# Linear attention and a max-of-three FFN on one core: k of batches 3 to 7 transposed by DMA, q's second chunk packed on ScalarE, batch 3's products a step later

## The chip, the cores and the metric

The kernel runs on one core of one Trainium2 chip. The metric is device microseconds of one execution. Times called "time" are these; a "span" is the length of one execution's trace, about 2 us, at most 3, shorter in these runs. A trace shows one execution. Times are compared within one call, on one chip, with the kernel before run in turn. A ratio is the mean time of one kernel's fast runs over the mean of the other's fast runs of the same rounds, so it is not quite the ratio of the medians that are quoted.

PE is the matmul engine and PEld its weight loads. DVE is VectorE, ACT is ScalarE, POOL is GpSimd and SP is SyncE. SP only issues DMAs here; SPq is its queue.

## The reference, cut to what matters

```python
# q, k, v: (8 batches, 8 heads, 1024, 64); E, F: (64, 1024)
k_proj = einsum('ks,bhsd->bhkd', E, k)          # 64 rows a head instead of 1024
v_proj = einsum('ks,bhsd->bhkd', F, v)
attn   = softmax(q @ k_proj^T / 8)              # (.., 1024, 64)
x      = (attn @ v_proj) as (8192 tokens, 512)
out    = max(x @ w1, x @ w2, x @ w3) @ w_out    # 512 -> 768 -> 512, float32
```

The FFN is nearly all of the PE work. The attention of batch n+1 is spread over the FFN steps of batch n.

## The kernel before

A batch has two chunks of 512 tokens. A chunk has ten steps: six `up` steps of 12 matmuls (about 2.6 us of PE each) and four `down` steps of 6 matmuls (1.3 us). `plan(b)` lists what attention work is put behind which step: `(1, 3)` is chunk 1, step 3. PE's work runs in the order of the program in these traces, so one instruction that waits holds up those that follow: in the changed kernel batch 4's first scores wait 3.25 us, and the `down` matmuls behind them start only after these, at 172.81 us instead of 169.68 before.

The kernel's scores read q and the projected k with the head dimension on the partitions. q gets there by a DMA transpose ("q's turn", 1 MB, issued by SP). k's projection gets there by two PE transposes and a copy out of PSUM:

```python
def load(b, which):                                   # on GpSimd's queue
    tiles = qkv[b] if b in qkv else load_tiles(b)
    for i in which:
        dma = nc.gpsimd.dma_start(out=tiles[i], in_=view((q, k, v)[i], b))
        if i == 0 and b - 1 in last_T:
            after(dma, last_T[b - 1])                 # q's load waits for the previous q turn

def qd(b, parts=1):                                   # pack q on VectorE, turn it by DMA
    def f():
        # ... allocation and packing copies cut
                last_T[b] = nc.sync.dma_start_transpose(out=qTs[b][...], in_=q_p[...])

def kproj(b):
    def f():
        t, ns = bank()
        proj(b, 1, t, (LO, HI), 4 * D)                # 16 matmuls
        kps[b] = att.tile([P, 2, 2 * D], BF16, name="kp")
        copy("v", kps[b].rearrange("a g x -> a (g x)"), t[:, 0:4 * D], ns, 0.43)

def kt(b):                                            # the transposes that the change removes
    def f():
        t, ns = two()
        t = t.bitcast(BF16)[:, 0]
        for gg in range(2):
            nc.tensor.transpose(out=t[:, gg * P:(gg + 1) * P],
                                in_=kps[b][:, gg, :], identity=ident)
        # ... a line cut
        kpTs[b] = att.tile([P, NPAIR, KP], BF16, name="kpT")
        copy("v", kpTs[b].rearrange("a (y x) k -> a x y k", x=2), t[...], ns, 0.3)

# qd: pack and turn q.  sc: scores of a head pair.  za, vx: sums, values.  zc: sums and 1/z, by SP DMAs
# plan(0), cut
(0, 7): [qd(1, 2), za(0, 2, *c1)],
(1, 2): [vproj(1), ld(2)],
# plan(2)
(0, 1): [kproj(3), vproj(3), ld(4)],
(0, 2): [kt(3)],
(0, 3): [sc(3, 0, now=True), sc(3, 1)],
(0, 5): [sc(3, 2, now=True), sc(3, 3)],
(0, 7): [zc(3)],
(0, 8): [qd(4)],
(1, 3): [kproj(4), vproj(4), ld(5), vx(3, 0), vx(3, 1)],
(1, 4): [kt(4)],
(1, 7): [vx(3, 2), vx(3, 3), sc(4, 0)],
# plan(3) and later, n = b + 1: the rest of n's scores at (0, 1), zc(n) at (0, 3), qd(n+1) at (0, 4),
# kproj(n+1), vproj(n+1) at (1, 2), kt(n+1), ld(n+2) at (1, 3), sc(n+1, 0) at (1, 6)
```

The softmax here doesn't subtract the row's maximum and nothing guards it: scores larger than these inputs give would overflow.

Of the kernel before, what the change touches and what calls it, by code (L numbers as in the profile page):

```python
# [9 lines left out]
BF16 = mybir.dt.bfloat16  # L10
# [5 lines left out]
def kernel(  # L16
# [13 lines left out]
    nc = tc.nc  # L30

    B, H, S, D = q.shape
    KP = E.shape[0]
# [4 lines left out]
    P = 128  # L38
# [13 lines left out]
    att = ctx.enter_context(tc.tile_pool(name="att", bufs=2))  # L52
# [55 lines left out]
    def after(dma, earlier):  # L108
        tc.add_manual_dep(
            dma.ins, earlier.ins.name,  # L110
            mybir.DependencyInfo(
                mybir.DependencyClass.Sync, mybir.DependencyReason.DATA
            ),
        )
# [16 lines left out]
    qkv, qTs, kpTs, vps, pTs, zis, xTs = {}, {}, {}, {}, {}, {}, {}  # L131
# [5 lines left out]
    def load_tiles(b):  # L137
        qkv[b] = tuple(
            loads.tile([P, H, SI, D], BF16, name=nm, bufs=n)
            for nm, n in (("q_t", 2), ("k_t", 1), ("v_t", 1))  # L140
        )
        return qkv[b]
# [55 lines left out]
    def load(b, which):  # L198
        tiles = qkv[b] if b in qkv else load_tiles(b)
        for i in which:  # L200
            dma = nc.gpsimd.dma_start(out=tiles[i], in_=view((q, k, v)[i], b))  # L201
            if i == 0 and b - 1 in last_T:
                after(dma, last_T[b - 1])

    def scores(b, g, lo, nsi):
        t, ns = two()
        n = nsi // 2
        for c in range(2):
            for hp in range(2):
                rows = slice(hp * HALF, (hp + 1) * HALF)  # L210
                at = g * SI + lo + c * n
                nc.tensor.matmul(  # L212
                    out=t[c * HALF:(c + 1) * HALF, hp, 0:n * P],
                    lhsT=kpTs[b][rows, g, :],
                    rhs=qTs[b][rows, at:at + n, :],
                    start=True, stop=True,
                )
        return t[:, :, 0:n * P], ns, pe(n * MM / 4 + 0.1)
# [65 lines left out]
    def vx(b, g):  # L284
        def f():
            scale_x(b, g, 0, SI, values(b, g, 0, SI))
        return f
# [34 lines left out]
    def sc(b, g, lo=0, nsi=SI, now=False):  # L322
        def f():
            t = scores(b, g, lo, nsi)
            if now:
                exps(b, g, lo, nsi, t)
            else:
                later.append(lambda: exps(b, g, lo, nsi, t))
        return f
# [34 lines left out]
    q_pk = {}  # L364

    def pack_q(b, gs, lo, nsi):


        def f():
            if b not in q_pk:  # L370
                q_pk[b] = att.tile([P, NPAIR, SI, 2, D], BF16, name="q_p", bufs=1)
            for g in gs:
                copy(
                    "v", q_pk[b][:, g, lo:lo + nsi].rearrange("p si h d -> p h si d"),
                    qkv[b][0][:, 2 * g:2 * g + 2, lo:lo + nsi], (), 0.25,
                )
        return f

# [39 lines left out]
    kps = {}  # L418
# [3 lines that stand above are left out]
            proj(b, 1, t, (LO, HI), 4 * D)  # L422
            kps[b] = att.tile([P, 2, 2 * D], BF16, name="kp")
            copy("v", kps[b].rearrange("a g x -> a (g x)"), t[:, 0:4 * D], ns, 0.43)
        return f

    def kt(b):
# [4 lines that stand above are left out]
                nc.tensor.transpose(  # L432
                    out=t[:, gg * P:(gg + 1) * P], in_=kps[b][:, gg, :], identity=ident
                )
            pe(0.2)

            kpTs[b] = att.tile([P, NPAIR, KP], BF16, name="kpT")
            copy(
                "v", kpTs[b].rearrange("a (y x) k -> a x y k", x=2),
                t[:, 0:2 * P].rearrange("a (x y k) -> a x y k", x=2, y=2), ns, 0.3,  # L440
            )
        return f

    def vproj(b):
        def f():
            t, ns = bank()
            proj(b, 2, t, (LO, HI), 4 * D)

            vps[b] = att.tile([P, H, D], BF16, name="vp")
            for hh, hs in enumerate((LO, HI)):  # L450
                i = t[hh * HALF:(hh + 1) * HALF, 0:4 * D].rearrange("a (h d) -> a h d", d=D)
                for to in range(2):
                    copy("sv"[hh], vps[b][to * HALF:(to + 1) * HALF, hs, :], i, ns, 0.4)
        return f
# [250 lines left out]
    def ld(b, which=(0, 1, 2)):  # L705
        return lambda: load(b, which)

    def plan(b):
        n = b + 1
        if b == 0:  # L710
            c1 = (SPC, SPC)
            return {
                (0, 6): [za(0, 1, *c1), sc(0, 3, *c1)],
                (0, 7): [qd(1, 2), za(0, 2, *c1)],
                (0, 8): [za(0, 3, *c1)],
                (1, 0): [kproj(1)],
                (1, 1): [kt(1)],
                (1, 2): [vproj(1), ld(2)],
                (1, (3, "mid")): [sc(1, 0, now=True), sc(1, 1)],
                (1, 4): [za(1, 0), sc(1, 2, now=True)],  # L720
                (1, 5): [za(1, 1), sc(1, 3)],
                (1, 7): [za(1, 2)],
                (1, 8): [za(1, 3)],
            }
        if b == 1:
            return {
                (0, 0): [qd(2)],
                (0, 3): [kproj(2), vproj(2), ld(3, (0,))],
                (0, 4): [kt(2)],
                (0, 5): [sc(2, 0, now=True), sc(2, 1, now=True), sc(2, 2)],  # L730
                (0, 6): [sc(2, 3)],
                (0, 8): [zc(2, nc.gpsimd), ld(3, (1, 2))],
                (1, 1): [qd(3)],
                (1, 3): [vx(2, 0), vx(2, 1)],
                (1, 6): [vx(2, 2), vx(2, 3)],
            }
        if b == 2:
            return {
                (0, 1): [kproj(3), vproj(3), ld(4)],
                (0, 2): [kt(3)],  # L740
                (0, 3): [sc(3, 0, now=True), sc(3, 1)],
                (0, 5): [sc(3, 2, now=True), sc(3, 3)],
                (0, 7): [zc(3)],
                (0, 8): [qd(4)],
                (1, 3): [kproj(4), vproj(4), ld(5), vx(3, 0), vx(3, 1)],
                (1, 4): [kt(4)],
                (1, 7): [vx(3, 2), vx(3, 3), sc(4, 0)],
            }
        if n == B:
            return {}  # L750
        out = {
            (0, 1): [sc(n, 1, now=True), sc(n, 2, now=True), sc(n, 3)],
            (0, 3): [zc(n)],
            (1, 2): [vx(n, 0), vx(n, 1)],
            (1, 6): [vx(n, 2), vx(n, 3)],
        }
        if n + 1 < B:
            out[0, 4] = [qd(n + 1)]
            out[1, 2] = [kproj(n + 1), vproj(n + 1)] + out[1, 2]
            out[1, 3] = [kt(n + 1)]  # L760
            out[1, 6] += [sc(n + 1, 0)]
        if n + 2 < B:
            out[1, 3] += [ld(n + 2)]
        return out

    for b in range(B):
        p = plan(b)

        def behind(ch, step):
            for f in p.get((ch, step), []):  # L770
                f()

        for ch in range(NCHUNK):
            if (b, ch) == (0, 0):
                c1 = (SPC, SPC)
                up_first({
                    (0, 0, 1): [lambda: x(1)],
                    (0, 0, 3): [lambda: z(2), lambda: z(3)],
                    (0, 1, 3): [lambda: v_pair(2), lambda: x(2)],
                    (0, 1, 5): [lambda: v_pair(3), ld(1)],  # L780
                    (0, 2, 1): [lambda: x(3)],
                    (2, "a", 0): [pack_q(0, (0, 1), *c1)],
                    (2, "a", 1): [pack_q(0, (2, 3), *c1)],
                    (2, "a", 4): [qp(0, (0, 1), *c1)],
                    (2, "a", 5): [qp(0, (2, 3), *c1)],
                    (2, 1): [sc(0, 0, *c1)],
                    (2, 3): [sc(0, 1, *c1)],
                    (2, 4): [za(0, 0, *c1, then=True), sc(0, 2, *c1)],
                })
                run_later()  # L790
                behind(0, NJT - 1)
            else:
                for step in range(NJT):
                    up(b, ch, step, lambda: behind(ch, (step, "mid")))
                    behind(ch, step)
            for tt in range(SPC):
                down(b, ch, tt, "v" if b == 0 else "s")
                behind(ch, NJT + tt)
# [30 lines left out]
```

## Time and profile before

| before | |
|---|---|
| time, median of 3 runs | 401.98 us (401.90 to 402.39) |
| span of the profiled run | 401.0 us |
| PE busy | 392.7 us, 98% |
| VectorE, ScalarE busy | 51%, 37% |
| chain that ended last, share on PE | 84% |

The windows view shows where PE is not busy. Columns: stretch in us from the span's start, its length, busy time of each engine (with the number of instructions), the granted PE clock as a share of full speed, DMA share, GB/s.

```profile
24.00:33.00 9.00, 9.00 (x43) 4.04 (x42) 6.25 (x11) 1.56 (x3) 1.66 (x2) 1.00 1.25 205
33.00:48.00 15.00, 14.08 (x111) 6.09 (x110) 12.17 (x24) 7.07 (x12) 0.00 (x0) 1.00 1.24 211
128.00:145.00 17.00, 16.29 (x104) 7.03 (x102) 8.35 (x16) 7.95 (x12) 2.63 (x3) 1.00 1.14 219
145.00:172.00 27.00, 26.92 (x166) 12.43 (x162) 14.30 (x20) 8.72 (x17) 2.33 (x3) 1.00 1.02 212
172.00:195.00 23.00, 23.00 (x122) 9.84 (x120) 9.55 (x16) 10.57 (x17) 0.30 (x1) 1.00 1.11 195
```

Between 24 and 381 us PE misses 0.92 us at 33 to 48, 0.71 us at 128 to 145, and little else. The second gap is the longest that a DMA causes after the start, by the list of waits (engine, line, releaser; total us, times, longest):

```profile
PE banks L346 <- DMA v_t<-in_v_dram: 0.7, 1, 0.7
```

What a k transpose pair costs PE shows in the timeline (start, us, engine, line, operation, count). Twelve matmuls from 251.37 us to 254.08 us take 2.71 us with the pair among them. The stream's pace of 0.216 us a matmul gives 2.59 us for twelve, so the pair takes 0.11 to 0.12 us:

```profile
251.37 2.76 PE L583 MATMUL banks<-xT,w_sb 128*128 128x512 bf16 x12
253.97 0.28 PE L432 MATMUL banks<-ident,kp 128*128 128x128 bf16 x2
254.08 1.24 PE L583 MATMUL banks<-xT,w_sb 128*128 128x512 bf16 x5
```

Batch 4: here are SP's queue and PE around its first scores (L212). The DMA issues view adds that q's turn needed 14.7 us from issue to landing, so it landed at 169.1 us:

```profile
151.71 2.61 SPq L276 DMA_DIRECT2D zi_all<-zd  x4
154.43 12.72 SPq L412 DMA_TRANSPOSE qT<-q_p  x1
167.25 2.72 SPq L701 DMA_DIRECT2D out_dram<-o_sb  x2
```

```profile
168.91 0.63 PE L232 MATMUL banks<-pT,vp 64*64 64x512 bf16 x8
169.37 0.39 PE L212 MATMUL banks<-qT,kpT 64*64 64x512 bf16 x4
169.68 2.76 PE L687 MATMUL banks<-wout_sb,hT 128*128 128x512 bf16 x12
172.28 5.34 PE L583 MATMUL banks<-xT,w_sb 128*128 128x512 bf16 x24
177.56 0.63 PE L212 MATMUL banks<-qT,kpT 64*64 64x512 bf16 x8
```

The second number in SP's lines is the time that the issue held SP's queue: 12.7 us for this turn. q's turn lands just as PE comes to use it. There is no wait, and no slack either.

### The profile page before, as it was taken

The page shows a single profiled execution, that of the slowest core. Times are in us where ns is not written, and L with a number is a line of the kernel's source. Part 1 is how long each engine was busy: PE and PEld are TensorE (multiplying, and loading weights), DVE is VectorE, ACT ScalarE, POOL GpSimd, SP SyncE. Part 2 cuts the span into 40 slices and gives each one's busy share as a digit, 9 for nine tenths or more (in the row PEclk, how much of TensorE's full clock was granted, in tenths as well). Part 3 has the DMA queues.
Part 4 walks back from the last instruction along what each step waited for, and adds up shares of the span by engine and source line. Part 5 has one row for each costly group of instructions (what it writes and reads, how often), then busy time and mean ns, then how long its engine had stood idle before and what let it go on. Part 6 is the DMA issues. An engine that isn't in the chain of part 4 may idle for free.

```text
span 401.0 us, 5752 instructions
## 1 busy us (share of the span) xinstructions
PE 392.7 (98%) x2286; PEld 176.6 (44%) x2286; DVE 204.1 (51%) x323; ACT 149.0 (37%) x238; POOL 34.4 (9%) x49
## 2 busy tenths in 40 slices
PE   8999999999999999999999999999999999999996
PEld 3444443353444435444454445444454444444443
DVE  2348756761673525746274544744267342745251
ACT  2532438527222452253323542245323533132322
POOL 7440002000400200010020000100000000000000
PEclk9999999999999999999999999999999999999999
DMA  9999999988899998999999959990980229020202
GB/s 154 206 206 207 231 201 145 227 157 158 209 176 209 215 227 181 206 190 210 222 224 172 245 130 268 184 244 24 203 217 1 106 66 253 0 105 2 105 0 105
DMA packets 66330, 66.09 MB, mean 165 GB/s; under 512 B 30624, under 2 KB 58784, under 8 KB 66304
## 3 DMA queue, kind: packets, MB, share of 16 engines
q0 software_dynamic: 29104, 30.41, 47.1%
q1 hardware_dynamic: 37056, 35.20, 34.8%
q8 instruction: 17, 0.28, 0.3%
q10 hardware_dynamic: 144, 0.13, 0.1%
q14 instruction: 9, 0.07, 0.1%
HBM read 69.73 MB, written 16.97 MB: 216 GB/s over the span
## 4 chain that ended last, share of the span: by engine, by line
PE 84%; DMA 8%; DVE 3%; ACT 2%; issue 2%; POOL 1%; DVEq 0%; POOLq 0%; ACTq 0%
PE banks L583 55%; PE banks L687 18%; DMA v_t<-in_v_dram 6%; PE banks L346 3%; PE banks L232 2%; PE banks L212 2%; DMA k_t<-in_k_dram 2%; DVE xT L309 1%; PE banks L257 1%; ACT zl L292 1%; DVE hT L593 1%; ACT zi_all L298 1%; PE banks L490 1%; DVE m L652 0%; PE banks L461 0%
## 5 line engine op out<-in xcount | busy, mean ns | idle before, releaser
L583 PE MATMUL banks<-xT,w_sb 128*128 128x512 bf16 x1152 | 257.6, 379 | 0.3 <-DVE xT L309 0.3
L583 PEld LDWEIGHTS <-w_sb 128*128 128x128 bf16 x1152 | 110.0, 98 | 136.1 <-issue 8.5
L652 DVE TENSOR_TENSOR m<-banks,h1s 128x512 f32<-128x512 f32 x90 | 62.1, 690 | 135.1 <-ACT h1s L648 93.2
L648 ACT COPY h1s<-banks 128x512 f32<-128x512 f32 x90 | 52.7, 586 | 119.2 <-PE banks L583 117.7
L687 PE MATMUL banks<-wout_sb,hT 128*128 128x512 bf16 x378 | 86.9, 380 | 0.1
L593 DVE TENSOR_TENSOR hT<-banks,m 128x512 bf16<-128x512 f32 x90 | 62.3, 692 | 10.1 <-DVE m L652 0.9
L687 PEld LDWEIGHTS <-hT 128*128 128x128 bf16 x378 | 35.2, 98 | 47.7 <-issue 5.8
L102 ACT COPY o_sb<-banks 128x512 f32<-128x512 f32 (+1 forms) x56 | 32.7, 583 | 57.8 <-PE banks L687 57.5
L223 ACT ACTIVATE pT<-banks 128x1024 bf16<-128x1024 f32 (+1 forms) x36 | 32.8, 931 | 26.5 <-PE banks L212 26.5
L309 DVE TENSOR_TENSOR xT<-banks,zi_all 128x1024 bf16<-128x1024 f32 x28 | 33.2, 1220 | 11.7 <-PE banks L232 6.9
L201 POOL DMA_DIRECT2D q_t<-in_q_dram x7 | 6.2, 880 | 194.8 <-DMA qT<-q_p 119.8
L102 DVE CAST vp<-banks 64x256 bf16<-64x256 f32 (+1 forms) x18 | 7.1, 397 | 12.4 <-ACT vp L102 9.3
L346 PEld LDWEIGHTS <-efT 128*64 128x64 bf16 x224 | 11.5, 110 | 4.4 <-issue 3.4
L102 ACT CAST vp<-banks 64x256 bf16<-64x256 f32 x14 | 5.1, 365 | 21.2 <-PE banks L346 21.1
L232 PE MATMUL banks<-pT,vp 64*64 64x512 bf16 (+1 forms) x144 | 11.5, 364 | 0.7 <-DVE vp L102 0.7
L212 PE MATMUL banks<-qT,kpT 64*64 64x512 bf16 (+1 forms) x144 | 11.2, 362 | 0.8 <-ACT zl L292 0.5
L102 DVE COPY q_p<-q_t 128x1024 bf16<-128x1024 bf16 (+1 forms) x32 | 11.3, 417 | 0.0
L292 ACT ACTIVATE zl<-banks 128x512 f32<-128x512 f32 (+1 forms) x12 | 8.9, 740 | 6.4 <-PE banks L232 5.9
L102 DVE COPY o_sb<-banks 128x512 f32<-128x512 f32 (+1 forms) x9 | 5.8, 653 | 4.5 <-PE banks L667 4.5
L461 PE MATMUL banks<-warm_f 128*128 128x512 f32 x8 | 6.6, 977 | 1.5 <-DVE warm_f L175 1.5
L346 PE MATMUL banks<-v_t,efT 128*64 128x256 bf16 x112 | 7.3, 273 | 0.7 <-DMA v_t<-in_v_dram 0.7
L346 PE MATMUL banks<-k_t,efT 128*64 128x256 bf16 x112 | 7.5, 276 | 0.0
(62 smaller groups left out, 119.3 us busy)
## 6 DMA issues: line engine op xcount, KB each, us to landing
out_dram<-o_sb SPq DMA_DIRECT2D x30, 512.0 KB, 4.4
zi_all<-zd SPq DMA_DIRECT2D x20, 512.0 KB, 7.9
q_t<-in_q_dram POOLq DMA_DIRECT2D x7, 1024.0 KB, 9.7
k_t<-in_k_dram POOLq DMA_DIRECT2D x7, 1024.0 KB, 17.2
v_t<-in_v_dram POOLq DMA_DIRECT2D x7, 1024.0 KB, 21.7
zi_all<-zd POOLq DMA_DIRECT2D x4, 512.0 KB, 8.3
w_sb<-in_moe_w_dram POOLq DMA_DIRECT2D x4, 384.0 KB, 11.3
k_t<-in_k_dram POOLq DMA_DIRECT2D x2, 512.0 KB, 8.7
```

Source lines behind the costliest of these rows:

```text
L102: done = {"v": nc.vector.tensor_copy, "s": nc.scalar.copy, "g": nc.gpsimd.tensor_copy}[eng](out=o, in_=i)
L212: nc.tensor.matmul(out=t[c * HALF:(c + 1) * HALF, hp, 0:n * P], lhsT=kpTs[b][rows, g, :], rhs=qTs[b][rows, at:at + n, :], start=True, stop ...
L223: nc.scalar.activation(out=pTs[b, g, lo], in_=t, func=AF.Exp, scale=scale)
L232: nc.tensor.matmul(out=t[hp * HALF:(hp + 1) * HALF, c, 0:nsi * HALF], lhsT=w(rows, hp), rhs=p[rows, hp, :], start=True, stop=True,)
L292: nc.scalar.activation(out=zl, in_=t, func=AF.Ln)
L309: nc.vector.tensor_tensor(out=xTs[b][:, g, lo:lo + nsi, :].rearrange("a (c s) p -> a c (s p)", c=2), in0=t, in1=zi, op=ALU.mult,)
L346: nc.tensor.matmul(out=t[hh * HALF:(hh + 1) * HALF, 0:width], lhsT=efT[:, si, (kv - 1) * KP:kv * KP], rhs=qkv[b][kv][:, heads[hh], si, :], ...
L583: nc.tensor.matmul(out=h, lhsT=w_sb[i][:, ct, jt * P:(jt + 1) * P], rhs=xTs[b][:, ct, ch * SPC:(ch + 1) * SPC, :], start=(ct == first), st ...
L593: nc.vector.tensor_tensor(out=o, in0=h, in1=other, op=ALU.max)
L648: nc.scalar.copy(out=h1s, in_=h[0][0])
L652: nc.vector.tensor_tensor(out=m12, in0=h[1][0], in1=h1s, op=ALU.max)
L687: nc.tensor.matmul(out=o_ps, lhsT=hTs[b, ch][:, jt, tt * P:(tt + 1) * P], rhs=wout_sb[:, jt, :], start=(jt == 0), stop=(jt == NJT - 1),)
```

## The change

Its intent is to take work from PE, which is busy 98% of the span, and to close the two gaps. k of batches 3 to 7 goes by a 64 KB DMA transpose on SP. q loads wait for the k turn of the batch before. Batch 0's second chunk of q is packed on ScalarE, and its transposes come earlier. Batch 3's products and first scores come a step later, so that v has landed. The diff is cut to what matters.

```diff
             if i == 0 and b - 1 in last_T:
                 after(dma, last_T[b - 1])
+            if i == 0 and b - 1 in turned:
+                after(dma, turned[b - 1])
@@ scores
-                    lhsT=kpTs[b][rows, g, :],
+                    lhsT=k_pair(b, g)[rows],          # the new tile's order of head pairs
@@ pack_q
-                    "v", q_pk[b][:, g, lo:lo + nsi]..., (), 0.25,
+                    "s", q_pk[b][:, g, lo:lo + nsi]..., (), 0.58,
@@
+    def kd(b):
+        def f():
+            kpTs[b] = att.tile([P, 2, 2 * KP], BF16, name="kpT2")
+            turned[b] = nc.sync.dma_start_transpose(
+                out=kpTs[b], in_=kps[b].rearrange("a g x -> a (g x)")
+            )
+        return f
@@ plan(2)
-                (0, 1): [kproj(3), vproj(3), ld(4)],
-                (0, 2): [kt(3)],
-                (0, 3): [sc(3, 0, now=True), sc(3, 1)],
+                (0, 2): [kproj(3), kd(3), vproj(3), ld(4)],
+                (0, 4): [sc(3, 0, now=True), sc(3, 1)],
-                (1, 3): [kproj(4), vproj(4), ld(5), vx(3, 0), vx(3, 1)],
-                (1, 4): [kt(4)],
+                (1, 3): [kproj(4), kd(4), vproj(4), ld(5), vx(3, 0), vx(3, 1)],
@@ plan(3) and later
-            out[1, 2] = [kproj(n + 1), vproj(n + 1)] + out[1, 2]
-            out[1, 3] = [kt(n + 1)]
+            out[1, 2] = [kproj(n + 1), kd(n + 1), vproj(n + 1)] + out[1, 2]
@@ batch 0's second chunk
-                    (2, "a", 4): [qp(0, (0, 1), *c1)],
+                    (2, "a", 3): [qp(0, (0, 1), *c1)],
-                    (2, 3): [sc(0, 1, *c1)],
+                    (2, 2): [sc(0, 1, *c1)],
```

More of the change, by code (lines that the diff above doesn't have):

```diff
@@ L203, in load, with k_pair @@
                 after(dma, last_T[b - 1])
+            if i == 0 and b - 1 in turned:
+                after(dma, turned[b - 1])
+    def k_pair(b, g):
+        if b in turned:
+            return kpTs[b][:, g % 2, (g // 2) * KP:(g // 2 + 1) * KP]
+        return kpTs[b][:, g, :]
+    turned = {}
     def scores(b, g, lo, nsi):
@@ L373, in f @@
                 copy(
-                    "v", q_pk[b][:, g, lo:lo + nsi].rearrange("p si h d -> p h si d"),
-                    qkv[b][0][:, 2 * g:2 * g + 2, lo:lo + nsi], (), 0.25,
+                    "s", q_pk[b][:, g, lo:lo + nsi].rearrange("p si h d -> p h si d"),
+                    qkv[b][0][:, 2 * g:2 * g + 2, lo:lo + nsi], (), 0.58,
                 )
@@ L758, in plan @@
             out[0, 4] = [qd(n + 1)]
-            out[1, 2] = [kproj(n + 1), vproj(n + 1)] + out[1, 2]
-            out[1, 3] = [kt(n + 1)]
+            out[1, 2] = [kproj(n + 1), kd(n + 1), vproj(n + 1)] + out[1, 2]
             out[1, 6] += [sc(n + 1, 0)]
         if n + 2 < B:
-            out[1, 3] += [ld(n + 2)]
+            out[1, 3] = [ld(n + 2)]
         return out
```

## The prediction

> **What bounds it now.** The engine table gives PE 392.7 of 401.0 us (98%), its clock row is all 9s, and the chain that ended last is 84% PE. By the windows, PE is idle only at the start and end (about 3 us each, untouched), at 33 to 48 us (0.92 us) and at 128 to 145 us (0.71 us). Only PE work, or those two gaps, can be won. VectorE (51%) and ScalarE (37%) don't bind.
>
> **Removed.** Two 128x128 PE transposes of k per batch, for batches 3 to 7. In the timeline 12 matmuls start at 251.37 us and the next 12, behind the pair, at 254.08; at the stream's 0.216 us they take 2.59, so the pair costs 0.11 us. Five pairs: 0.55 us. Five 0.28 us VectorE copies go too, off the chain.
>
> **Batch 3 a step later.** Its v projection waited 0.71 us for v, landing at 128.7 us (waits, issues). A step is 2.6 us, so this goes: -0.7 us.
>
> **Front.** q's second chunk lands near 31.7 us (issue 19.49, landing 12.2), but VectorE packs it only at 32.82 (4 x 0.28 us), behind six maxima. ScalarE is idle from 26.6 to 36.4 us; its 128x512 copies take 0.586 us, so packing ends near 34.1, pair by pair ahead of need, and VectorE's PSUM copies and maxima start about 0.4 us sooner: -0.4 us.
>
> **Added.** Each k turn is 64 KB, 1/16 of a q turn. The least disturbed q turn took SP 5.5 us to issue and 7.4 to land: about 0.35 and 2.2 us for k (estimates). In batches 5 to 7 q's turn is issued before k's product is ready, and scores come about 9 us later: hidden. Batch 4 is the danger. SP issues its q turn from 154.43 to 167.15 us; it lands at 169.1, and the scores that need it begin at 169.2 to 169.4, without slack. k's turn stands behind it on SP. [...] So k lands near 170 us, while PE, ahead by 1.3 us, would arrive near 168.
>
> Batch 4's q load also now waits for batch 3's k turn, so its three loads start near 134 instead of 131.3 us and overlap the zi broadcasts and q's turn; a 2.3 us DMA hole near 152 us hides most of this. I expect PE to wait 1 to 2.5 us at batch 4's first scores, or partly at its v projection, which gives back most of the gains so far. Gains after it: 0.33 us.
>
> **Sum.** -0.4 -0.7 -0.55 +1.2: about 401.5 us. Range 400.1 to 403.3. Faster by over 2%: 1%; within 2%: 97%; slower: 2%.
>
> **What would show it.** PE records: 10 transposes fewer. Waits: none for v at batch 3; a new one of 1 to 2.5 us for qT or the transposed k at batch 4's first scores. Groups: q_p copies of 128x512 on ScalarE near 0.59 us. SP timeline: batch 4's k turn directly after q's long one. Windows: 33 to 48 us at least 0.3 us less idle. Issues: batch 4 loads 2 to 3 us later.
>
> **What would make it wrong.** If batch 4's turns land before PE comes, the time is near 400.3. If v of batch 4, now sharing the DMA engines, is much later, or k turns cost several us each, it is 403 to 405. Batch 3's scores, nearer together, may cost 0.2 us; another deal of PSUM banks, a few tenths either way.

The landing of k "near 170 us" was the author's estimate: q's turn leaves SP at 167.15 us, and the estimated 2.2 us from issue to landing give 169.4 at the earliest. From the 401.98 us before, the four terms come to 401.5.

## The result, and the profile after

The changed kernel takes 407.19 us (406.08 to 408.44, 4 runs) against 402.19 us before (4 runs), ratio 1.0124 (1.0089 to 1.0158). It is slower by 1.2%. That is within 2%, as predicted, but 5 us, outside the predicted range. The profiled run has a span of 405.7 us, 4.7 us more than before's.

The same five windows after:

```profile
24.00:33.00 9.00, 8.95 (x44) 4.03 (x42) 5.95 (x10) 2.67 (x6) 1.75 (x2) 1.00 1.25 205
33.00:48.00 15.00, 14.57 (x113) 6.57 (x114) 11.86 (x21) 8.15 (x15) 0.00 (x0) 1.00 1.24 214
128.00:145.00 17.00, 16.89 (x114) 7.60 (x115) 7.57 (x13) 8.13 (x13) 2.63 (x3) 1.00 0.92 177
145.00:172.00 27.00, 23.84 (x142) 11.01 (x142) 15.22 (x23) 7.71 (x14) 0.00 (x0) 1.00 1.15 222
172.00:195.00 23.00, 22.21 (x109) 9.38 (x113) 9.34 (x16) 9.49 (x14) 2.63 (x3) 0.93 1.04 185
```

Both old gaps are nearly closed: 0.92 became 0.43 us and 0.71 became 0.11. A new one of 3.2 us stands in 145 to 172, and in the last window PE's clock is 0.93 of full speed. The list of waits names the new gap, and a second new one of 1.0 us:

```profile
PE banks L221 <- DMA kpT<-kp: 3.2, 1, 3.2
PE banks L355 <- DMA v_t<-in_v_dram: 1.0, 1, 1.0
```

The second is not the old wait for batch 3's v, which is gone. It is batch 1's v projection. Before, PE had 12 matmuls there and no wait (first fence, before); after, the same matmuls come 0.43 us sooner and then PE waits (second fence, after):

```profile
53.04 2.75 PE L583 MATMUL banks<-xT,w_sb 128*128 128x512 bf16 x12
55.72 1.06 PE L346 MATMUL banks<-v_t,efT 128*64 128x256 bf16 x16
```

```profile
52.61 2.75 PE L600 MATMUL banks<-xT,w_sb 128*128 128x512 bf16 x12
56.34 1.06 PE L355 MATMUL banks<-v_t,efT 128*64 128x256 bf16 x16 [0.98 <-DMA v_t<-in_v_dram]
```

At batch 4, SP's queue and PE after:

```profile
152.31 2.61 SPq L285 DMA_DIRECT2D zi_all<-zd  x4
155.03 13.77 SPq L421 DMA_TRANSPOSE qT<-q_p  x1
168.90 0.53 SPq L718 DMA_DIRECT2D out_dram<-o_sb  x1
169.52 1.37 SPq L456 DMA_TRANSPOSE kpT<-kp  x1
```

```profile
168.59 0.63 PE L241 MATMUL banks<-pT,vp 64*64 64x512 bf16 x8
172.46 0.41 PE L221 MATMUL banks<-qT,kpT 64*64 64x512 bf16 x4 [3.25 <-DMA kpT<-kp]
172.81 1.35 PE L704 MATMUL banks<-wout_sb,hT 128*128 128x512 bf16 x3
174.38 2.88 PE L704 MATMUL banks<-wout_sb,hT 128*128 128x512 bf16 x8 [0.22 <-issue]
177.09 1.24 PE L600 MATMUL banks<-xT,w_sb 128*128 128x512 bf16 x5
```

The reader should see three things here. First, k's turn is issued after q's long one and after an output store that stands between them in program order. It landed 2.9 us later, at 172.4. Second, q's turn itself (15.8 us from issue to landing) came at 170.8 us, 1.7 us later than before. So about half of the 3.25 us would have been a wait for q. Third, the matmuls that follow the wait are slow: the trace has eleven from 172.81 to 177.09 us, where twelve took 169.68 to 172.28 before. (There are probably twelve here too: this trace lacks some matmul records, and a gap of 0.22 us stands in the stretch.) The windows show why. These are before and then after, 1 us each:

```profile
173.00:174.00 1.00, 1.00 (x6) 0.42 (x5) 0.00 (x0) 0.18 (x1) 0.00 (x0) 1.00 0.90 67
```

```profile
173.00:174.00 1.00, 1.00 (x3) 0.35 (x3) 0.00 (x0) 0.00 (x0) 0.96 (x2) 0.50 0.40 160
```

The clock was granted at one half. The trace's clock records give this stretch 3.413 us, from 172.96 to 176.37, so it costs 1.7 us at full speed's pace.

Where the 4.7 us arose can be followed by the start of the same PE work in both traces:

| work | before, us | after, us | after minus before |
|---|---|---|---|
| k projection of batch 1 | 49.33 | 48.90 | -0.43 |
| v projection of batch 1 | 55.72 | 56.34 | +0.62 |
| sums of batch 3 | 144.29 | 143.89 | -0.40 |
| last values of batch 3, just before batch 4's first scores | 168.91 | 168.59 | -0.32 |
| batch 4's other scores | 177.56 | 182.37 | +4.81 |
| k projection of batch 5 | 202.50 | 207.30 | +4.80 |
| k projection of batch 7 | 295.52 | 300.11 | +4.59 |

This run of after started 0.46 us late, since its first k load landed later (10.10 against 9.64 us). It was 0.43 us ahead at batch 1's k projection all the same, so the front gained about 0.9 us. Batch 1's v took that back. Batch 3's step and its transposes gained 1.0 us. Batch 4's first scores then cost 5.1 us: 3.25 of waiting, 1.7 of slow clock, and 0.2 that I don't account for. From batch 5 to 7 two periods gain 0.21 us together, as predicted for the transposes. The chain view (start, us, what) has those periods, first before and then after:

```profile
202.50 1.87 PE banks L346 x32
249.01 1.87 PE banks L346 x32
295.52 1.87 PE banks L346 x32
```

```profile
207.30 1.87 PE banks L355 x32
253.71 1.87 PE banks L355 x32
300.11 1.87 PE banks L355 x32
```

ScalarE packs as expected. The groups view (count, busy us, mean ns, idle before) shows it starting as q lands and keeping near the 0.59 us estimate:

```profile
L102 ACT COPY q_p<-q_t 128x512 bf16<-128x512 bf16 x4 | 2.2, 615 | 4.9 <-DMA q_t<-in_q_dram 4.9
```

### The profile page after: what moved, and what is told of

Read it like the earlier page. It is cut to its first block, busy times and chain, and to the rows that moved or that the text cites. A ratio compares the mean times of both kernels' runs of the same rounds, so it can differ in the third digit from the quotient of the medians.

```text
span 405.7 us, 5697 instructions
## 1 busy us (share of the span) xinstructions
PE 389.7 (96%) x2234; PEld 176.6 (44%) x2276; DVE 202.6 (50%) x314; ACT 151.1 (37%) x242; POOL 34.4 (8%) x49
## 3 DMA queue, kind: packets, MB, share of 16 engines
q0 software_dynamic: 29104, 30.41, 46.4%
## 4 chain that ended last, share of the span: by engine, by line
PE 79%; DMA 14%; ACT 2%; DVE 2%; issue 2%; POOL 0%; SPq 0%; DVEq 0%; ACTq 0%; POOLq 0%
PE banks L600 52%; PE banks L704 18%; DMA v_t<-in_v_dram 7%; PE banks L355 3%; PE banks L241 2%; DMA zi_all<-zd 2%; DMA k_t<-in_k_dram 2%; PE banks L221 2%; DMA zd<-zic 1%; DVE xT L318 1%; PE banks L266 1%; ACT zl L301 1%; DMA kpT<-kp 1%; ACT zi_all L307 1%; PE banks L507 0%
## 5 line engine op out<-in xcount | busy, mean ns | idle before, releaser
L600 PE MATMUL banks<-xT,w_sb 128*128 128x512 bf16 x1119 | 254.1, 379 | 2.5 <-issue 0.8
L102 DVE COPY q_p<-q_t 128x1024 bf16<-128x1024 bf16 x28 | 10.4, 435 | 3.2 <-DMA q_t<-in_q_dram 3.2
L221 PEld LDWEIGHTS <-kpT 64*64 64x64 bf16 x144 | 3.7, 105 | 10.5 <-issue 4.6
```

Source lines behind the costliest of these rows:

```text
L102: done = {"v": nc.vector.tensor_copy, "s": nc.scalar.copy, "g": nc.gpsimd.tensor_copy}[eng](out=o, in_=i)
L221: nc.tensor.matmul(out=t[c * HALF:(c + 1) * HALF, hp, 0:n * P], lhsT=k_pair(b, g)[rows], rhs=qTs[b][rows, at:at + n, :], start=True, stop= ...
L600: nc.tensor.matmul(out=h, lhsT=w_sb[i][:, ct, jt * P:(jt + 1) * P], rhs=xTs[b][:, ct, ch * SPC:(ch + 1) * SPC, :], start=(ct == first), st ...
```

## The experiments

The theory, called A: batch 4's k turn comes too late, PE waits for it, and the wait then halves the clock (0.50 for 3.413 us in the trace above); nothing else in the change costs anything worth naming. Rivals: B, each k turn costs SP and DMA time, and batch 4 is only where it shows; C, the loss comes from the front or from batch 3's later step; D, the loads that now start later (134.7 us for batch 4's q against 131.3) make batch 4's turns late. All outputs are right.

### k_only: the k turns alone

From the kernel before, only the k turns and the q loads' waits for them; the front and batch 3's step stay as before.

```diff
@@ on the kernel before, besides kd, k_pair and the waits of the q loads; batches 5 to 7 alike
-                (0, 1): [kproj(3), vproj(3), ld(4)],
-                (0, 2): [kt(3)],
+                (0, 1): [kproj(3), kd(3), vproj(3), ld(4)],
-                (1, 3): [kproj(4), vproj(4), ld(5), vx(3, 0), vx(3, 1)],
-                (1, 4): [kt(4)],
+                (1, 3): [kproj(4), kd(4), vproj(4), ld(5), vx(3, 0), vx(3, 1)],
```

> The kernel before, with the k turns of batches 3 to 7 by DMA and the waits of the q loads that belong to them, and nothing else of the change (no front, no later step). If batch 4's k turn carries the whole loss: a PE wait of 2 to 3.5 us at batch 4's first scores, 403.5 to 407 us, no wait at batch 3's scores worth naming. If the loss needs the three parts together, the time is within 1 us of before.

Measured: 407.44 us (407.04 to 407.63, 4 runs), ratio 1.0117 (1.0095 to 1.0139). Its wait at batch 4's first scores:

```profile
171.31 0.58 PE L221 MATMUL banks<-qT,kpT 64*64 64x512 bf16 x4 [2.55 <-DMA kpT<-kp]
```

The wait is in the range expected, the time just above it. All four runs have a mean clock of 0.994 to 0.996. The k turns alone bring the whole loss, so C falls. Its wait is shorter than the changed kernel's, but its time is the same: by the mean clock, the slow stretch came in every run here (one was profiled).

### front_only and step_only: the other two parts alone

```diff
@@ front_only, on the kernel before
-                    "v", q_pk[b]..., (), 0.25,
+                    "s", q_pk[b]..., (), 0.58,
-                    (2, "a", 4): [qp(0, (0, 1), *c1)],
+                    (2, "a", 3): [qp(0, (0, 1), *c1)],
-                    (2, 3): [sc(0, 1, *c1)],
+                    (2, 2): [sc(0, 1, *c1)],
@@ step_only, on the kernel before
-                (0, 1): [kproj(3), vproj(3), ld(4)],
-                (0, 2): [kt(3)],
-                (0, 3): [sc(3, 0, now=True), sc(3, 1)],
+                (0, 2): [kproj(3), vproj(3), ld(4)],
+                (0, 3): [kt(3)],
+                (0, 4): [sc(3, 0, now=True), sc(3, 1)],
```

> The kernel before, with the front's part of the change alone (packing on ScalarE, q's transposes and the second scores a step earlier). In three runs of the changed kernel PE reached batch 1's k projection 0.9 to 1.0 us sooner than before where the start was even, and then waited 1.0 to 1.4 us for batch 1's v load, which before it did not. Theory (the gain is real on PE but the load of v, and not PE, sets when batch 1's v projection runs): the same here, a wait for v of batch 1 of about 1 us, and the time within 0.5 us of before. Rival (the v wait comes from the rest of the change): no such wait, the time 0.8 to 1.0 us below before.

Measured: 402.95 us (6 runs), ratio 1.0010 (0.9994 to 1.0025). The wait for batch 1's v is there without the rest of the change:

```profile
56.61 1.06 PE L346 MATMUL banks<-v_t,efT 128*64 128x256 bf16 x16 [1.13 <-DMA v_t<-in_v_dram]
```

So the front's gain is real on PE, and DMA takes it back 20 us later. The front neither gains nor loses.

> The kernel before, with batch 3's k and v projections, transposes and first scores a step later and nothing else. The wait of 0.7 us for v at batch 3 goes and the PE records from batch 3 on come 0.7 to 1.0 us sooner, until batch 4's first scores, where q's turn lands near 169 us: there PE waits 0.5 to 1 us for it. So the time stays within 0.5 us of before. Rival (q's turn comes sooner with PE): the time is 0.7 to 1.0 us below before.

Measured: 402.84 us (5 runs), ratio 1.0000 (0.9986 to 1.0014). In its trace there is no wait for v at batch 3, and none for q's turn at batch 4's first scores either, which start at 168.50 us. There my expectation was wrong: the turn moved with PE. The profiled span is 400.1 us, 0.9 below before's. Yet the five spans average 400.6 us against 400.7 for before. So one trace shows the gain, and the times do not. The other traces say why it may be missing: the wait is not in every run. With batch 3's step left where it was, before's trace has 0.71 us of it and front_only's 0.34, but k_only's and front_qd_later's have none. In front_qd_later PE comes to batch 3's v at 127.97 us, and v is there; in before it landed only at 128.8:

```profile
127.97 1.04 PE L346 MATMUL banks<-v_t,efT 128*64 128x256 bf16 x16
```

So the 0.71 us that the prediction read from one trace was not a fixed cost.

### k4_on_pe: one k turn undone

```diff
@@ on the changed kernel
-                (1, 3): [kproj(4), kd(4), vproj(4), ld(5), vx(3, 0), vx(3, 1)],
+                (1, 3): [kproj(4), vproj(4), ld(5), vx(3, 0), vx(3, 1)],
+                (1, 4): [kt(4)],
```

> After, but batch 4's k alone is transposed on PE again (batches 3, 5, 6, 7 stay on DMA). Theory A (batch 4's k turn comes too late, and the PE wait then halves the clock): the PE wait at batch 4's first scores shrinks from 3.2 us to what q's own turn leaves, at most 1.7 us; no half-clock stretch there; time 401 to 403. Rival B (every k turn costs SP and DMA time, batch 4 is only where it shows) or rival C (front or batch 3's later step is the loss): time stays above 405.

Measured: 403.14 us (402.44 to 405.54, 4 runs), ratio 1.0031 (0.9994 to 1.0067). One of the four runs, 405.54 us at a full clock, was not profiled, and I cannot explain it. In the trace the wait is for q's turn, and it is 0.5 us; no slow stretch follows (the clock is 1.00 from 172 to 195 us):

```profile
169.36 0.41 PE L221 MATMUL banks<-qT,kpT 64*64 64x512 bf16 x4 [0.50 <-DMA qT<-q_p]
```

Four k turns stay on DMA and cost nothing to see, though the interval of the ratio leaves room for 2.7 us; score4_later, next, leaves less. As the cause of the whole loss B falls. One turn of five makes it.

### score4_later: the same turn, used later

```diff
@@ on the changed kernel, plan(2)
-                (1, 7): [vx(3, 2), vx(3, 3), sc(4, 0)],
+                (1, 7): [vx(3, 2), vx(3, 3)],
@@ plan(3)
+            (0, 0): [sc(4, 0)] if n == 4 else [],
```

> After, but batch 4's first scores stand 3 steps of the schedule later (batch 3's first step in place of batch 2's second-chunk first down step), all else the same, all five k turns on DMA. Theory A: the PE wait vanishes (below 0.3 us), clock 1.0 throughout, time 401 to 402.5. Rivals B and C: above 405, the wait only moves.

Measured: 403.01 us (402.81 to 403.64, 4 runs), ratio 1.0013 (0.9998 to 1.0028). The wait is gone, and so is the slow stretch (the profiled run has a mean clock of 0.999, and twelve matmuls from 171.94 us take 2.7):

```profile
174.62 0.41 PE L221 MATMUL banks<-qT,kpT 64*64 64x512 bf16 x4
```

The time is half a us above what I expected. The trace has a likely reason: PE waited 1.4 us for batch 1's v, the front's give-back. All five turns by DMA cost nothing that shows (the interval reaches 0.28%, 1.1 us) once nothing needs batch 4's before 174.6 us.

### fill_pe: work in place of the wait

Twelve useless matmuls, 2.6 us of PE, stand just before batch 4's first scores.

```diff
@@ on the changed kernel, plan(2)
-                (1, 7): [vx(3, 2), vx(3, 3), sc(4, 0)],
+                (1, 7): [vx(3, 2), vx(3, 3), lambda: idle(12), sc(4, 0)],
```

> After, with 12 useless matmuls (2.6 us of PE) just before batch 4's first scores, where PE waited 3.2 us. Theory A says that 1.7 us of the loss is the clock granted at one half for 3.4 us after that idle time: the wait shrinks below 1 us, the half-clock stretch is gone, and the time falls by 1 to 2 us to about 405.5 although work was added. If the clock has nothing to do with the idle time, the stretch stays and the time is 407 or more.

Measured: 404.82 us (404.47 to 405.40, 4 runs), ratio 1.0057 (1.0042 to 1.0072); the changed kernel had 1.0124 and 1.0102. They were run at other times. Added work made it faster by about 2 us (1.8 to 2.7 by these ratios). PE kept busy, and the `down` matmuls behind the scores run at full pace, twelve in 2.6 us:

```profile
169.35 2.76 PE L478 MATMUL banks<-warm 128*128 128x512 bf16 x12
172.05 0.41 PE L221 MATMUL banks<-qT,kpT 64*64 64x512 bf16 x4
172.39 2.76 PE L704 MATMUL banks<-wout_sb,hT 128*128 128x512 bf16 x12
```

So the slow clock here comes with the wait (fill_pe has 1.00 from 172 to 195 us, the changed kernel 0.93) and is a cost of its own. By its mean clock no run of fill_pe has the slow stretch (0.998 to 1.0). A slow clock may come without this wait too: one of the eleven runs of before in the call of k_only and after_again, not profiled, has a mean clock of 0.994 and a span of 402.2 us. The clock records of the traces of before and of the changed kernel hold two values only, 1.0 and 0.5. In the changed kernel's the clock is full for 167.253 us, half for 3.413 us, full again for 228.693 us, and half in the last 0.7 us; in before's it is full for 395.946 us, to the kernel's end. Shorter waits than the changed kernel's 3.25 us were followed by half clock too: 2.55 us in k_only (0.50 from 173 to 174 us) and 1.93 us in kd4_first, next. Those of 0.50 us (k4_on_pe) and 0.86 us (no_turn_wait) were not: 1.00 from 172 to 195 us in both traces. What decides whether a wait is followed by the slow stretch was not shown.

### kd4_first: k's turn issued ahead of q's

Batch 4's k product comes two steps earlier. SP gets its turn first and q's turn right after it.

```diff
@@ on the changed kernel, plan(2); held=True packs q and leaves the turn to turns[4]
-                (0, 8): [qd(4)],
-                (1, 3): [kproj(4), kd(4), vproj(4), ld(5), vx(3, 0), vx(3, 1)],
+                (0, 8): [qd(4, held=True)],
+                (1, 1): [kproj(4), kd(4), lambda: turns[4]()],
+                (1, 3): [vproj(4), ld(5), vx(3, 0), vx(3, 1)],
```

> After, with batch 4's k product and turn two steps earlier and issued by SP ahead of q's long turn; q's turn is issued where it was (near 155 us). If k's place behind q's turn on SP[...] is what makes it late, k lands before 160 us, and the remaining wait at batch 4's first scores is for q's turn alone: 1 to 2 us, no half-clock stretch, time 402 to 404.5. If the later loads make both turns late alike, the wait stays near 3 us and the time near 407.

Measured: 405.08 us (404.32 to 406.25, 4 runs), ratio 1.0064 (1.0043 to 1.0086). The wait is now for q's turn, as expected:

```profile
170.94 0.41 PE L221 MATMUL banks<-qT,kpT 64*64 64x512 bf16 x4 [1.93 <-DMA qT<-q_p]
```

Three expectations failed. The time is above the 404.5 us expected at most. k did not land before 160 us: issued at 155.62 us right behind zi's four broadcasts and a store, its 64 KB needed 11.8 us. Batch 3's, in the changed kernel, with one output store still under way before it and no loads, needed 2.3 us. In this place the small transfer's landing went with that of what stood before it: the store, issued at 154.98 us, took 12.2 us and landed at 167.2, and k landed at 167.4. What made both late was not shown. And the half-clock stretch (0.50 from 172.5 to 175 us) came after an idle time of only 1.93 us. In the other three runs of this kernel the mean clock was 0.999 to 1.0. So a wait of this length can be followed by the slow stretch; how long the others waited was not profiled.

### no_turn_wait: the loads not held back

```diff
@@ on the changed kernel, load
-            if i == 0 and b - 1 in turned:
-                after(dma, turned[b - 1])
```

> After, without the wait of each q load for the k turn of the batch before (the loads of batch 4 then start near 131.5 us, not 134.7). If the later loads are what makes batch 4's turns late (my prediction gave them a part), q's turn of batch 4 lands 1 to 2 us sooner, the PE wait there falls to 1 to 2 us and the time to 403 to 405. If k's place behind q's turn is all of it, the wait and the time stay as after. A k turn that runs beside loads may take longer than 2.3 us; batch 3's has about 3 us to spare.

Measured: 404.35 us (403.92 to 406.63, 6 runs), ratio 1.0056 (1.0036 to 1.0077). Batch 4's q load is issued at 131.2 instead of 134.7 us, its q turn lands at 168.9 instead of 170.8, k's turn 1.9 us sooner, and the wait falls from 3.25 to 0.86 us, without a slow stretch (1.00 from 172 to 195 us):

```profile
170.54 0.41 PE L219 MATMUL banks<-qT,kpT 64*64 64x512 bf16 x4 [0.86 <-DMA kpT<-kp]
```

So D holds for its part: both things make the turn late, the loads held back and k's place behind q. The price of dropping the wait shows at batch 3, whose k turn now runs beside the loads. It takes 6.6 us instead of 2.3, and PE waits 0.95 us for it.

### after_again: the changed kernel once more

No edit.

> The changed kernel once more, unaltered, beside the other runs of this call on one chip, and to see how often the half-clock stretch comes. Expected: 406 to 408, ratio to before 1.010 to 1.015, a PE wait of 3 to 3.5 us at batch 4's first scores in the trace; its executions fall in two groups about 2 us apart, with a mean clock of 0.995 to 0.996 in the slower ones and 0.999 or 1.0 in the others.

Measured: 407.10 us (404.26 to 409.11, 6 runs), ratio 1.0102 (1.0066 to 1.0138); the trace has a wait of 3.47 us at batch 4's first scores. Of the ten runs of the changed kernel, six have a mean clock of 0.993 to 0.995 and a mean span of 405.8 us, and four have 0.998 or 0.999 and 403.6 us. The groups are less clean than I expected: one of the six has a span of only 404.3 us. Their difference of 2.2 us is near the 1.7 us of the stretch. So a good part of the kernel's spread probably comes from there.

### score4_v1_later, front_qd_later, score4_b1_later: room at the front too

Three ways to keep the front's gain from being taken back at batch 1.

```diff
@@ score4_v1_later: score4_later, and in plan(0)
-                (1, 2): [vproj(1), ld(2)],
+                (1, 3): [vproj(1), ld(2)],
@@ front_qd_later: front_only, and in plan(0)
-                (0, 7): [qd(1, 2), za(0, 2, *c1)],
-                (0, 8): [za(0, 3, *c1)],
+                (0, 7): [za(0, 2, *c1)],
+                (0, 8): [qd(1, 2), za(0, 3, *c1)],
@@ score4_b1_later: score4_v1_later, and in plan(0)
-                (1, (3, "mid")): [sc(1, 0, now=True), sc(1, 1)],
-                (1, 4): [za(1, 0), sc(1, 2, now=True)],
-                (1, 5): [za(1, 1), sc(1, 3)],
+                (1, (4, "mid")): [sc(1, 0, now=True), sc(1, 1)],
+                (1, 5): [za(1, 0), sc(1, 2, now=True)],
+                (1, 6): [za(1, 1), sc(1, 3)],
```

> After, with both waits given room: batch 4's first scores three steps later, and batch 1's v projection a step (2.6 us) later. If the two waits for DMA are what keeps the change from paying, neither is there (each below 0.3 us), the half-clock stretch is gone, and PE's earlier times survive to the end: about 1.2 us below the run with the later scores alone, 400.8 to 401.8, and faster than before by 0.5 to 1.5 us. If another wait takes their place, the time stays at 402 to 403.

Measured: 401.96 us (5 runs), ratio 0.9988 (0.9974 to 1.0002). Both waits are gone, but PE now waits 0.53 us for batch 1's q turn, as a third gate. The time is just above the 400.8 to 401.8 us expected. A small gain is likely and not certain.

> Front alone, with q's packing and turn of batch 1 one down step (about 1.7 us) later. In seven traces with the front part, q's turn of batch 1 started at 43.8 to 44.5 us and v of batch 1 landed at 55.8 to 56.8; in two without it, 44.8 and 55.2 to 55.3. If the earlier turn takes DMA time from v's load, then with the turn at 45 us or later v lands at 55.4 or sooner and PE's wait for it falls to 0.5 us or less (PE may then wait for q's turn at the first scores instead). If v lands near 56 all the same, the cause is another. Time within 0.7 us of before either way.

Measured: 402.14 us (401.93 to 402.16, 4 runs), ratio 0.9983 (0.9964 to 1.0001). q's turn started at 46.4 us (44.5 in front_only), and PE's wait for v fell to 0.26 us:

```profile
55.77 1.06 PE L346 MATMUL banks<-v_t,efT 128*64 128x256 bf16 x16 [0.26 <-DMA v_t<-in_v_dram]
```

v landed at 55.8 us, sooner than front_only's 56.6 but not by 55.4 as the theory asked. That q's earlier turn takes DMA time from v's load is supported by this and not settled.

> The version with both waits given room, and batch 1's scores, sums and values of pairs 0 and 1 a step later too, since its first scores waited 0.5 us for q's turn of batch 1. If that wait is the last one in the way: no DMA wait over 0.2 us from 24 us on, and 0.2 to 0.6 us below the version with the scores in place, 401.3 to 402.2, against before -0.5 to -1.2 us.

Measured: 402.60 us (6 runs), ratio 0.9998 (0.9982 to 1.0014). A miss: the DMA waits are gone, and PE waits 1.4 us for ScalarE's exponentials of batch 1, in two places, which now come too late.

### both_room and both_room_pe: is there anything to gain?

Both gates given room: q's turn of batch 1 and batch 4's first scores later. One has k on DMA, the other has it on PE in the same schedule (the front and batch 3's step included).

```diff
@@ both_room: score4_later, and in plan(0)
-                (0, 7): [qd(1, 2), za(0, 2, *c1)],
-                (0, 8): [za(0, 3, *c1)],
+                (0, 7): [za(0, 2, *c1)],
+                (0, 8): [qd(1, 2), za(0, 3, *c1)],
@@ both_room_pe: the same schedule with kt(3), kt(4), kt(n + 1) in place of kd, no waits for turns
```

> The changed kernel (k on DMA) with the two gates given room in the way that worked best alone: batch 1's q turn one down step later, batch 4's first scores three steps later. If the prediction's gains (front, batch 3's step, 0.55 us of transposes) are real once neither gate holds PE: no DMA wait over 0.3 us after 24 us, span 399.0 to 399.8 us in the trace, time 400.8 to 401.8, 1 to 2 us below before. If there is a further cost of the k turns, it stays near before.

> The same schedule with k transposed on PE in all batches, so without the added DMA turns and without the q loads' waits for them. Against the run with the turns, on the same chip: 0.3 to 0.7 us longer if the removed transposes are worth the predicted 0.55 us; equal or shorter if the turns cost as much elsewhere (SP, DMA share, loads that start later).

Measured: both_room 402.27 us (401.42 to 403.95, 6 runs), ratio 0.9995 (0.9977 to 1.0012). both_room_pe 402.32 us (401.74 to 403.06, 6 runs), ratio 0.9991 (0.9979 to 1.0003). The profiled run of both_room, its fastest, has a span of 399.6 us with no DMA wait over 0.3 us after 24 us, as hoped. Its median is above the 400.8 to 401.8 us expected: other runs of it reach 402.0 us at a full clock. Those were not profiled, and what held them up is open. Between the two kernels no difference shows: the 0.55 us of removed transposes is smaller than the spread of the runs. No version was found that clearly beats the kernel before.

## Why the prediction was wrong

The step that failed is the one that the prediction gave as "I expect PE to wait 1 to 2.5 us at batch 4's first scores, or partly at its v projection, which gives back most of the gains so far", with the term "+1.2" in the sum. The place and the mechanism of the wait were right; its size was not, and a second cost, the slow clock, was left out. The term measured 4.95 us: 3.25 us of waiting, and 1.7 us of half clock that the prediction did not have at all.

- **The wait, 3.25 instead of about 1.2 us.** The prediction took k to land "near 170 us" and PE to come near 168, which is 2 us already; the sum has 1.2. PE came at 169.2, and k landed at 172.4. q's turn landed at 170.8 rather than 169.1, because the loads started 3.4 us later; no_turn_wait shows that this is worth about 1.9 us. An output store stood between the two turns on SP (0.53 us of SP; what it cost was not run apart); I had not read SP's program order closely enough to see it. And the estimate of 0.35 us of SP and 2.2 us to land, scaled from the 1 MB turn, was too low: 1.4 and 2.9 us in this place, and 1.2 to 2.2 us of SP and 2.3 to 5.0 us to land over the five turns. Scaling by size failed.
- **The clock, 1.7 us, missing.** fill_pe shows it: with PE kept busy the clock is 1.00 from 172 to 195 us (0.93 in the changed kernel), and the time falls although work is added. In k_only it came in every run, by the mean clock (0.994 to 0.996).
- **The front, predicted -0.4 us.** PE gained about 0.9 us by batch 1's k projection, and lost it at batch 1's v projection, where v's load sets the pace. front_only: net zero. The prediction looked at one gap and not at what the earlier PE would meet next. In before's trace, v's load landed 29.4 us after its issue at 25.79, at 55.2 us, and PE came at 55.72: half a us of slack. That could have been read.
- **Batch 3's step, predicted -0.7 us.** The wait is gone from the trace, but the times of step_only show no gain. The wait was read from one trace, and two others without the later step do not have it (k_only, front_qd_later).
- **The transposes, predicted -0.55 us.** Right at 0.11 us a batch (periods of 46.51 and 46.40 us), and too small to see in any time.
- **"In batches 5 to 7 ... hidden".** Right: no waits there, and score4_later and k4_on_pe keep those turns without cost.
- **"If batch 4's turns land before PE comes, the time is near 400.3".** Not so: score4_later, where they do, took 403.01 us, in part because the front's gain was already lost (1.4 us of waiting in its trace).

## What to carry to other kernels

PE was 98% busy here, and much of the rest was timed to arrive just before PE needed it (q's turn for batch 4 landed at 169.1 us, and PE came at 169.4). In such a kernel work taken from the engine may only move it into the next DMA gate, as the 3.25 us wait here; read the slack of each later landing before counting the gain. Put new small DMAs where nothing long stands ahead of them in their queue: the same 64 KB landed in 2.3 us with one output store under way before it, and in 11.8 us behind four broadcasts and a store (kd4_first). Waits of 1.93, 2.55 and 3.25 us in the middle of the PE stream were followed by a stretch at half clock in the traces of kd4_first, k_only and the changed kernel, worth 1.7 us in the last; so count it in. Move the consumer before you try to speed up the producer: moving batch 4's scores by three steps repaired what the change broke (403.01 us against 407.19). Nothing here made the change pay.

## What was measured of the clock and of the turns

- The clock: PE waits of 1.93 us (kd4_first, one of four runs) and 2.55 us (k_only, four of four by their mean clock) were followed by half clock. In the changed kernel's trace the stretch is 3.413 us long, which costs 1.7 us. The changed kernel, with waits of 3.25 and 3.47 us in its two traces, shows the slow stretch by its mean clock in six of ten runs.
- The q turns, 1 MB from SBUF to SBUF: 7.4 us from issue to landing at best in before's trace (batch 2's turn; 1,048,576 bytes in 7.4 us are 142 GB/s, with the transfer's start and completion in it), 6.7 us at best in the changed kernel's, and 12.7 to 23.0 us in before's for the later batches, beside other traffic. How fast the same copy would be without the transpose was not run.
- A q turn held SP for most of the transfer's time: 4.9 to 19.7 us for batches 2 to 7 in the changed kernel. What stands behind it there started after that: at batch 4 q's turn left SP at 168.80 us, the store came at 168.90 and k's turn at 169.52, though k's product had been copied out of PSUM by 159.5.
- The k turns, 64 KB: they held SP for 1.2 to 2.2 us and landed in 2.3 to 5.0 us in the changed kernel, in 6.6 us beside three loads (no_turn_wait, batch 3) and in 11.8 us behind four broadcasts and a store (kd4_first, batch 4).
